# Sinkhorn attention into a gated MLP on one core: all of q turned on TensorE in bf16, eight shared load buffers, a new order of units

## The chip, the core and the metric

The kernel runs on one core of a Trainium2 chip. Five engines work side by side, each on its own queue of instructions: TensorE (PE in the profile, with its weight loads on a row of their own, PEld), VectorE (DVE), ScalarE (ACT), GpSimd (POOL) and SyncE (SP, which here only issues DMAs). The metric is the device time of one execution in microseconds (us); lower is better.

## What is computed

```python
# attention: batch 4, 8 heads, 768 rows, 64 columns; sort_net gives one 8x8 matrix per head
P = sort_net
for _ in range(5):                                   # five Sinkhorn rounds
    P = exp(P - max);  P /= sum over rows;  P /= sum over columns
k_sorted = einsum('bhij,bhjcd->bhicd', P, k_blocks)  # 8 blocks of 96 rows, mixed by P
v_sorted = einsum('bhij,bhjcd->bhicd', P, v_blocks)
attn = softmax(q_blocks @ k_sorted.T / 8)            # inside a block: 96 x 96
x = (attn @ v_sorted) as (4, 768, 512)               # the 8 heads side by side
# gated MLP with a spatial unit
h = relu(x @ w_in)                                   # 512 -> 1024
u, v = h[..., :512], h[..., 512:]
v_n = (v - mean) / sqrt(var + 1e-6)
v_s = einsum('ts,bsd->btd', w_spatial, v_n) + b_spatial
out = (u * v_s) @ w_out                              # float32, (4, 768, 512)
```

## The kernel before

The work of the four batches is cut into small *units*, each a function `u_XX`, and the text table `ORDER` (lines 18 to 51) lists every unit in the order in which its instructions are written. Nothing reorders them afterwards: each engine runs its own instructions in this order, and waits between engines are by semaphore. So a unit's place in `ORDER` settles what stands ahead of it on each of the five queues. A unit such as `SC:2:1:0:1` names, after the operation, the PSUM tile that it writes (there are four, `ps0` to `ps3`, of two banks each), the engine that empties it where there is a choice (A for ACT, D for DVE, P for POOL), the batch and the piece. A unit that writes a PSUM tile waits until the tile's last user has emptied it.

The units, in the order of one batch's data:

- `L` loads from DRAM, issued by POOL, with a cast to bf16: `q`, `k` and `v` of a batch (768 KB in bf16 each; batch 0 in two halves), the two halves of `w_in` (`wv`, `wu`), `w_spatial` (`ws`) and `w_out` (`wo`). Each of `q`, `k` and `v` has two buffers of its own. At most eight of POOL's DMAs are in flight: the ninth waits for the first to land.
- `SK` is one Sinkhorn round (DVE and ACT), `PR`, `P0`, `PC` and `PD` spread the result into the mixing matrices `pd`. `DM` runs matmuls on a tile of zeros ahead of the first data.
- `QT` turns two heads of q (128 x 768) to `qT`: twelve matmuls against the identity into an fp32 PSUM tile, and a copy. This is done for batches 0 and 1. For batches 2 and 3, `QP` first copies q into another order (`qp`, one buffer, on POOL or DVE), and `QX` turns all eight heads with one DMA transpose, issued by SP.
- `KT` mixes and turns k; `VT` and `VB` mix, turn and turn back v of batch 0; for batches 1 to 3, `VM` mixes v into the one tile `vm`, and `VC` has SP copy it by eight DMAs into `vb` (two buffers).
- `SC` computes scores of two heads and four blocks, with the exp on ACT; `AT` multiplies them by `vb`, and DVE normalizes into `x_sb`.
- `XT` (PE, batches 0 and 1) or `XD` (a DMA transpose, batches 2 and 3) turns the attention's output to `xT`.
- `VP` and `UP` are the two halves of `x @ w_in`; `ST`, `LN` and `LA` are the layer norm of v on DVE (with two small operations on ACT); `WT` turns `w_spatial`; `SP` is the spatial product, whose result DVE adds to the bias (`z`); `GT` multiplies by u (POOL or DVE); `OP` is the last product, `OE` empties it and `OS` stores it.
- `CK`, `CF` and `LF` compute and read one flag that says whether the inputs need the general path, a second version of the whole program behind a branch at the end, which is not taken here. `BH` marks the place of a branch hint.

Of the kernel before, what the change touches and what calls it, by code (L numbers as in the profile page):

```python
# [65 lines left out]
def kernel(  # L66
# [12 lines left out]
    nc = tc.nc  # L79
# [19 lines left out]
    ld = ctx.enter_context(tc.tile_pool(name="ld", bufs=2))  # L99
# [54 lines left out]

    def u_L(what, *a):
        if what in ("q", "k", "v"):
            b, lo, hi = (int(x) for x in a)
            src = {"q": q, "k": k, "v": v}[what]  # L160
            if (what, b) not in st:
                st[what, b] = ld.tile([128, H, G * D], BF16, name=f"{what}_in", tag=what)
# [4 lines left out]
        elif what == "wv":  # L167
            nc.gpsimd.dma_start(
                out=w_in_sb[:, :, DH:DFF], in_=moe_w_in.rearrange("(kc p) f -> p kc f", p=128)[:, :, DH:DFF])
        elif what == "wu":  # L170
            nc.gpsimd.dma_start(
                out=w_in_sb[:, :, 0:DH], in_=moe_w_in.rearrange("(kc p) f -> p kc f", p=128)[:, :, 0:DH])
        elif what == "ws":
            nc.gpsimd.dma_start(out=wsp_nat, in_=moe_w_spatial.rearrange("(c p) s -> p c s", p=128))
        elif what == "wo":
            nc.gpsimd.dma_start(out=w_out_sb, in_=moe_w_out.rearrange("(fc p) n -> p fc n", p=128))
# [112 lines left out]
    def natural(eng, dst, t):  # L289
        copy(eng, dst[:, 0:S].rearrange("p (x g) -> p x g", g=G), t[:, 0:S].rearrange("p (g x) -> p x g", g=G))  # L290
# [96 lines left out]
    def s_block(bank, ii, in_runs):  # L387
        if in_runs:
            return bank[:, 0:HW].rearrange("p (g x) -> p g x", g=G)[:, :, ii * TB:(ii + 1) * TB]
        return bank[:, ii * BLK:(ii + 1) * BLK]  # L390

    def u_SC(ps, b, hp, ih):
# [3 lines left out]
        for ii in range(NI):  # L396
            i = ih * NI + ii
            for hh in range(2):
                rows = slice(hh * 64, hh * 64 + 64)
                nc.tensor.matmul(  # L400
                    s_block(t[:, hh], ii, ("qp", b) in st),
                    lhsT=kT[rows, i * BLK:i * BLK + 128], rhs=q_block(b, hp, rows, i),
                    start=True, stop=True,
                )
        e, scores = e_tile(b, hp, ih), t[0:BLK, :, 0:NI * BLK]
        if ("qp", b) in st:
            e = e.rearrange("p h (x g) -> p h x g", g=G)
            scores = scores.rearrange("p h (g x) -> p h x g", g=G)
        nc.scalar.activation(out=e, in_=scores, func=AF.Exp, scale=scale)  # L409
# [307 lines left out]
```

## Time and profile before

| what | value |
|---|---|
| time before, median of 3 runs | 171.51 us (171.31 to 175.47) |
| the profiled execution | 171.02 us, of which the profile's span is 169.2 us |
| PE busy | 147.8 us (87%) |
| DVE, ACT, POOL busy | 118.3, 81.4, 43.9 us |
| loaded from DRAM, stored | 24.78 MB, 6.29 MB |

The span starts with the first instruction and ends with the last; some 1.8 us of the execution lie outside it. "Idle before" in the profile is the time that an engine stood still ahead of an instruction, with what it waited for behind the arrow. PEclk is the clock that TensorE was granted, as a share of full speed. `SPq` or `DVEq` means the engine's queue, not its work. The page of the profile merges matmuls that follow each other: `x12` is twelve of them.

### The profile page before, as it was taken

What the parts mean: (1) busy time and instruction counts of PE and PEld (TensorE: products, weight loads), DVE (VectorE), ACT (ScalarE), POOL (GpSimd) and SP (SyncE); (2) the same over time, 40 slices, a digit from 0 to 9 for tenths busy, and PEclk for the clock granted to TensorE, in tenths of its full rate; (3) what the DMA queues carried; (4) which work ended last, traced back from release to release, by engine and by line L of the source; (5) the groups of instructions that cost most, each with busy time, mean ns of one, the idle gap of its engine ahead of it and who ended that gap; (6) DMA issues with size and microseconds to landing.
All of it is one profiled execution on the core that took longest, in us unless ns stands there. A gap on an engine that the chain in (4) does not pass through costs nothing.

```text
span 169.2 us, 3790 instructions
## 1 busy us (share of the span) xinstructions
PE 147.8 (87%) x1559; PEld 90.8 (54%) x1559; DVE 118.3 (70%) x261; ACT 81.4 (48%) x113; POOL 43.9 (26%) x49
## 2 busy tenths in 40 slices
PE   7828989999799899819689999999999999999840
PEld 5627867765576666413255655555566545555310
DVE  3855699889599936149478697868959689546630
ACT  3227696796776653304737343688650045600120
POOL 7957320000009945318000030000003600006000
PEclk9995699999999999975999999999999999999996
DMA  2999999999996999914999926891309903311063
GB/s 24 173 195 204 208 205 203 207 212 205 248 267 98 120 158 157 113 17 53 188 254 224 204 48 34 242 237 28 124 6 114 318 0 124 124 62 67 4 252 128
DMA packets 33589, 24.74 MB, mean 146 GB/s; under 512 B 13472, under 2 KB 30368, under 8 KB 33568
## 3 DMA queue, kind: packets, MB, share of 16 engines
q0 software_dynamic: 14896, 12.19, 47.5%
q1 hardware_dynamic: 18672, 12.28, 32.9%
q8 instruction: 13, 0.21, 0.5%
q14 instruction: 8, 0.07, 0.1%
HBM read 24.78 MB, written 6.29 MB: 184 GB/s over the span
## 4 chain that ended last, share of the span: by engine, by line
PE 49%; DMA 24%; DVE 10%; ACT 6%; issue 3%; SPq 2%; POOL 2%; DVEq 0%; ACTq 0%; POOLq 0%
PE ps L558 12%; PE ps L584 10%; DMA qT<-qp 10%; PE ps L546 8%; DMA vb<-vm 7%; PE ps L503 7%; DMA v_in<-in_v_dram 6%; PE ps L336 3%; PE ps L448 3%; PE ps L400 3%; DVE v_sb L532 2%; DVE x_sb L456 2%; ACT ex L409 2%; SPq L376 2%; DVE z L564 2%
## 5 line engine op out<-in xcount | busy, mean ns | idle before, releaser
L574 POOL TENSOR_TENSOR gt<-z,u_sb 128x768 bf16<-128x768 f32 x10 | 16.4, 1641 | 76.4 <-DVE rec_all L455 46.4
L558 PE MATMUL ps<-wspT,v_sb 128*128 128x384 bf16 x192 | 33.0, 326 | 0.1
L409 ACT ACTIVATE ex<-ps 96x768 bf16<-96x768 f32 x32 | 24.3, 806 | 9.0 <-PE ps L400 9.0
L558 PEld LDWEIGHTS <-v_sb 128*128 128x128 bf16 x192 | 18.2, 98 | 11.8
L503 PE MATMUL ps<-w_in_sb,xT 128*128 128x512 bf16 x96 | 24.1, 400 | 0.0
L546 PE MATMUL ps<-xT,w_in_sb 128*128 128x384 bf16 x128 | 23.3, 326 | 0.6 <-DVE x_sb L456 0.6
L564 DVE TENSOR_TENSOR z<-ps,b_bc 128x768 f32<-128x768 f32 x16 | 15.3, 955 | 11.9 <-PE ps L558 11.9
L584 PE MATMUL ps<-w_out_sb,gt 128*128 128x512 bf16 x96 | 22.7, 381 | 0.7 <-DVE gt L574 0.7
L456 DVE TENSOR_TENSOR x_sb<-ps,rec_all 96x512 bf16<-96x512 f32 x32 | 22.0, 687 | 1.1
L110 ACT COPY o_sb<-ps 128x1024 f32<-128x1024 f32 (+1 forms) x11 | 9.7, 895 | 21.9 <-PE ps L584 18.2
L116 ACT ACTIVATE v_sb<-ps 128x1024 bf16<-128x1024 f32 x8 | 8.2, 1023 | 23.5 <-PE ps L503 23.5
L520 DVE BATCH_NORM_STATS2 stats<-v_sb 128x6 f32<-128x512 bf16 x24 | 16.2, 674 | 1.0 <-ACT v_sb L116 0.9
L546 PEld LDWEIGHTS <-w_in_sb 128*128 128x128 bf16 x128 | 11.6, 98 | 8.4 <-DVE x_sb L456 1.1
L448 PE MATMUL ps<-vb,ex 96*128 96x65 bf16 x256 | 12.5, 193 | 3.1 <-DMA vb<-vm 3.0
L503 PEld LDWEIGHTS <-xT 128*128 128x128 bf16 x96 | 9.4, 101 | 10.8 <-issue 1.7
L584 PEld LDWEIGHTS <-gt 128*128 128x128 bf16 x96 | 8.9, 98 | 11.3 <-DVE gt L574 1.1
L448 PEld LDWEIGHTS <-ex 96*128 96x128 bf16 x256 | 10.7, 97 | 6.9 <-issue 3.3
L116 ACT ACTIVATE u_sb<-ps 128x768 bf16<-128x768 f32 x13 | 10.5, 811 | 7.3 <-PE ps L546 7.3
L400 PE MATMUL ps<-qT,kt 64*128 64x96 bf16 x256 | 10.1, 215 | 4.6 <-DVE z L564 4.1
L400 PEld LDWEIGHTS <-kt 64*128 64x128 bf16 x256 | 7.0, 100 | 9.8 <-issue 5.2
L110 ACT CAST kt<-ps 128x768 bf16<-128x768 f32 x12 | 9.2, 803 | 5.9 <-PE ps L336 5.9
L314 POOL COPY qp<-q_in 128x768 bf16<-128x768 bf16 x5 | 4.2, 871 | 28.4 <-DMA q_in<-in_q_dram 28.4
(89 smaller groups left out, 181.8 us busy)
## 6 DMA issues: line engine op xcount, KB each, us to landing
out_dram<-o_sb SPq DMA_DIRECT2D x9, 512.0 KB, 3.6
vb<-vm SPq DMA_DIRECT2D x24, 99.0 KB, 5.4
k_in<-in_k_dram POOLq DMA_DIRECT2D x3, 768.0 KB, 18.4
q_in<-in_q_dram POOLq DMA_DIRECT2D x3, 768.0 KB, 20.8
v_in<-in_v_dram POOLq DMA_DIRECT2D x3, 768.0 KB, 16.4
out_dram<-o_sb SPq DMA_DIRECT2D x6, 256.0 KB, 2.5
wsp_nat<-in_moe_w_spatial_dram POOLq DMA_DIRECT2D x1, 1152.0 KB, 26.6
w_in_sb<-in_moe_w_in_dram POOLq DMA_DIRECT2D x2, 512.0 KB, 14.1
```

The lines of the kernel that those rows point to most:

```text
L110: nc.scalar.copy(out=out, in_=in_)
L116: nc.scalar.activation(out=out, in_=in_, func=AF.Relu)
L400: nc.tensor.matmul(s_block(t[:, hh], ii, ("qp", b) in st), lhsT=kT[rows, i * BLK:i * BLK + 128], rhs=q_block(b, hp, rows, i), start=True, ...
L409: nc.scalar.activation(out=e, in_=scores, func=AF.Exp, scale=scale)
L448: nc.tensor.matmul(t[:, hh, ii * VW:ii * VW + D + 1], lhsT=e[:, c:c + 128], rhs=vb[b % 2][:, ih * NI + ii, 2 * hp + hh, 0:D + 1], start=Tr ...
L456: nc.vector.tensor_mul(out=x_sb[:, hp].rearrange("p i (h d) -> p h i d", h=2), in0=tv[:, :, :, 0:D], in1=_raw_ap(rec, 0, [rec.ap[0], [NI, ...
L503: nc.tensor.matmul(t[:, x, :], lhsT=st["xT", b][:, n // 3, kc, (n % 3) * 128:(n % 3 + 1) * 128], rhs=w_in_sb[:, kc, DH:DFF], start=(kc == ...
L546: nc.tensor.matmul(t[:, x, 0:HW], lhsT=w_in_sb[:, kc, mc * 128:(mc + 1) * 128], rhs=st["xT", b][:, ih, kc, :], start=(kc == 0), stop=(kc = ...
L558: nc.tensor.matmul(t[:, x, 0:HW], lhsT=st["v_sb", b, n][:, mc * 128:(mc + 1) * 128], rhs=wspT[:, 3 * x:3 * x + 3, n, :], start=(n == 0), s ...
L564: nc.vector.tensor_add(out=z.rearrange("p (x c) -> p x c", x=2), in0=t[:, :, 0:HW], in1=b_bc.rearrange("p (x c) -> p x c", x=2),)
L574: eng.tensor_mul(out=gt, in0=st["z", b, mc], in1=st["u", b, mc // 2][:, mc % 2])
L584: nc.tensor.matmul(t[:, x, :], lhsT=st["gt", b, mc][:, (n0 + x) * 128:(n0 + x + 1) * 128], rhs=w_out_sb[:, mc, :], start=(mc == 0), stop=( ...
```

## The change

1. **q.** `QP` and `QX` are used no more. All of q is turned on TensorE, with transposes that write bf16 to PSUM: `QT` for two heads (batch 0), and the new `QQ` for four heads at once, whose copy is 128 x 1536 (batches 1 to 3). All of `SC` now reads q in the order that only batches 2 and 3 had.
2. **Load buffers.** The pool `ld` has eight equal buffers, taken in turn by whatever is loaded: q, k and v of all batches, and `w_spatial`, which is loaded in two halves (`wsa`, `wsb`) and has no tile of its own any more. Batch 0's q, k and v are loaded whole.
3. **Copies in two parts.** `KT` may have its copy done half by DVE and half by ACT (`DA`, `AD`).
4. **Order.** `ORDER` is another: among much else v of batch 1 is loaded ahead of k and q, `SC` and `AT` of a batch stand elsewhere, 9 of the 16 `GT` are on DVE (6 before), the warm-up matmuls are 36 of 512 columns (34 of 256 before), and `CK`, `CF` and `LF` stand at the very end. The attention's output of batches 2 and 3 is turned by DMA as before, one `XD` per half.

```diff
-    ld = ctx.enter_context(tc.tile_pool(name="ld", bufs=2))
+    ld = ctx.enter_context(tc.tile_pool(name="ld", bufs=8))
...
-    wsp_nat = const.tile([128, G, S], BF16, name="wsp_nat")
...
+    def ld_tile(name):
+        return ld.tile([128, H, G * D], BF16, name=name, tag="ld")
...
     def natural(eng, dst, t):
-        copy(eng, dst[:, 0:S].rearrange("p (x g) -> p x g", g=G), t[:, 0:S].rearrange("p (g x) -> p x g", g=G))
+        to = dst[:, 0:S].rearrange("p (x g) -> p x g", g=G)
+        of = t[:, 0:S].rearrange("p (g x) -> p x g", g=G)
+        for n, e in enumerate(eng):
+            x = slice(n * 128 // len(eng), (n + 1) * 128 // len(eng))
+            copy(e, to[:, x], of[:, x])
...
+    def q_turned(t, b, hp):
+        for g in range(G):
+            for hh in range(2):
+                nc.tensor.transpose(
+                    t[hh * 64:hh * 64 + 64, g * 128:(g + 1) * 128],
+                    st["q", b][:, 2 * hp + hh, g * D:(g + 1) * D], ident)
+
     def u_QT(ps, eng, b, hp):
+        b, hp = int(b), int(hp)
+        t = ps_tile(ps, BF16)
+        q_turned(t[:, 0], b, hp)
+        copy(eng, q_tile(b)[:, hp * S:(hp + 1) * S], t[:, 0, 0:S])
+
+    def u_QQ(ps, eng, b, hp):
+        b, hp = int(b), int(hp)
+        t = ps_tile(ps, BF16)
+        for x in range(2):
+            q_turned(t[:, x], b, hp + x)
+        copy(eng, q_tile(b)[:, hp * S:(hp + 2) * S].rearrange("p (k c) -> p k c", k=2), t[:, :, 0:S])
...
 ORDER = """
-CO S0 L:q:0:0:4 IV:0 IV:1 ID DM:0:18:256 L:k:0:0:4 SK:0 MA SK:1 MB L:q:0:4:8 IV:2 L:k:0:4:8 DM:1:16:256 SK:2 MC SK:3
+S0 CO SK:0 L:q:0:0:8 L:k:0:0:8 L:v:0:0:8 L:v:1:0:8 BH SK:1 SK:2 L:k:1:0:8 ID IV:2 MC IV:0 DM:1:6:512 L:q:1:0:8 SK:3
...
```

Three places show how this moves instructions.

SP's queue, from the start of the program. `vb<-vm` are the eight DMAs of one `VC`, `qT<-qp` is a `QX`, `xT<-x_sb` an `XD`, `out_dram<-o_sb` an `OS`. Before:

```order
L179 DMA p_all<-in_sort_net_dram 32x64
L376 DMA vb_99<-vm 96x1x528 x8
L185 DMA b_bc<-in_moe_b_spatial_dram 128x768
L321 DMA_TRANSPOSE qT<-qp 128x24x128
L376 DMA vb_98<-vm 96x1x528 x8
L599 DMA out_dram<-o_sb 128x2x512
L466 DMA_TRANSPOSE xT<-x_sb 128x16x96
L321 DMA_TRANSPOSE qT<-qp 128x24x128
```

The same queue after the change:

```order
L182 DMA p_all<-in_sort_net_dram 32x64
L403 DMA vb_98<-vm 96x1x528 x8
L188 DMA b_bc<-in_moe_b_spatial_dram 128x768
L403 DMA vb_97<-vm 96x1x528 x8
L610 DMA out_dram<-o_sb 128x2x512
L486 DMA_TRANSPOSE xT<-x_sb 128x16x96
L610 DMA out_dram<-o_sb 128x2x512
L403 DMA vb_98<-vm 96x1x528 x8
```

Both DMA transposes of q are gone, and nothing stands between the bias and the eight copies of batch 2; the first `XD` now stands ahead of all eight copies of batch 3.

DVE's queue around the spatial product of batch 0 and the mixing of batch 2's v. `qp<-q_in` is a `QP` of batch 3, `z` the emptying of an `SP`, `vm` that of a `VM` of batch 2. Before:

```order
L564 TENSOR_TENSOR z<-ps_1306,b_bc 128x768
L520 BN_STATS stats<-v_sb 128x6
L521 BN_AGGR mv<-stats 128x2
L314 COPY qp<-q_in 128x2x6x64
L564 TENSOR_TENSOR z<-ps_1344,b_bc 128x768
L112 CAST vm<-ps_1365 128x2x6x64
L314 COPY qp<-q_in 128x2x6x64
```

The same place after the change:

```order
L575 TENSOR_TENSOR z<-ps_1222,b_bc 128x768
L109 CAST kt_107<-ps_1249 128x384
L109 CAST kt_108<-ps_1264 128x384
L109 CAST kt_104<-ps_1279 128x384
L109 CAST vm<-ps_1346 128x2x6x64
L575 TENSOR_TENSOR z<-ps_1350,b_bc 128x768
```

The copies into `qp`, which had to wait until the DMA transpose of batch 2 had read the only `qp` buffer, are gone from ahead of `z` and `vm`.

ACT's queue where batch 2's and batch 3's v are mixed, after the change: the first two `vm` rows are the last two of batch 2, and the next two belong to batch 3.

```order
L107 CAST vm<-ps_1369 128x2x6x64
L107 CAST vm<-ps_1384 128x2x6x64
L427 ACTIVATE ex_101<-ps_1403 96x768
L427 ACTIVATE ex_102<-ps_1413 96x768
L113 ACTIVATE v_sb<-ps_1438 128x1024
L427 ACTIVATE ex_103<-ps_1449 96x768
L427 ACTIVATE ex_99<-ps_1459 96x768
L113 ACTIVATE u_sb<-ps_1472 128x2x384
L107 CAST vm<-ps_1500 128x2x6x64
L107 CAST vm<-ps_1504 128x2x6x64
L107 COPY o_sb<-ps_1508 128x1024
```

Before, sixteen other ACT instructions stood between the last `vm` of batch 2 and the first of batch 3 on this queue; now there are six. Since `vm` is one tile, the first `vm` row of batch 3 waits until all eight copies `vb<-vm` of batch 2 have landed.

More of the change, by code (lines that the diff above doesn't have):

```diff
@@ L138 @@
     eps_tile = const.tile([128, 1], FP32, name="eps")
-    warm = const.tile([128, 256], BF16, name="warm")
+    warm = const.tile([128, 512], BF16, name="warm")
     w_in_sb = const.tile([128, KC, DFF], BF16, name="w_in_sb")
-    wsp_nat = const.tile([128, G, S], BF16, name="wsp_nat")
     wspT = const.tile([128, G, G, 128], BF16, name="wspT")
@@ L161, in u_L @@
             if (what, b) not in st:
-                st[what, b] = ld.tile([128, H, G * D], BF16, name=f"{what}_in", tag=what)
+                st[what, b] = ld_tile(f"{what}_in")
             nc.gpsimd.dma_start(
@@ L172, in u_L @@
                 out=w_in_sb[:, :, 0:DH], in_=moe_w_in.rearrange("(kc p) f -> p kc f", p=128)[:, :, 0:DH])
-        elif what == "ws":
-            nc.gpsimd.dma_start(out=wsp_nat, in_=moe_w_spatial.rearrange("(c p) s -> p c s", p=128))
+        elif what in ("wsa", "wsb"):
+            c0 = 0 if what == "wsa" else G // 2
+            st["ws", c0 // (G // 2)] = w = ld_tile("ws_in").rearrange("p h c -> p (h c)")[:, 0:G // 2 * S].rearrange(
+                "p (c s) -> p c s", s=S)
+            nc.gpsimd.dma_start(
+                out=w, in_=moe_w_spatial.rearrange("(c p) s -> p c s", p=128)[:, c0:c0 + G // 2])
         elif what == "wo":
@@ L312, in u_QP @@
         if ("qp", b) not in st:
-            st["qp", b] = att.tile([128, HP, G, 2, D], BF16, name="qp", tag="qp", bufs=1)
+            st["qp", b] = ld_tile("qp").rearrange("p h c -> p (h c)").rearrange(
+                "p (k g h d) -> p k g h d", k=HP, g=G, h=2)
         getattr(nc, {"P": "gpsimd", "D": "vector"}[eng]).tensor_copy(
@@ L400, in u_SC @@
                 nc.tensor.matmul(
-                    s_block(t[:, hh], ii, ("qp", b) in st),
-                    lhsT=kT[rows, i * BLK:i * BLK + 128], rhs=q_block(b, hp, rows, i),
+                    t[:, hh, 0:HW].rearrange("p (g x) -> p g x", g=G)[:, :, ii * TB:(ii + 1) * TB],
+                    lhsT=kT[rows, i * BLK:i * BLK + 128], rhs=q_runs(b, hp, rows, i),
                     start=True, stop=True,
                 )
[L405 to L409, printed above, removed]
+        nc.scalar.activation(
+            out=e_tile(b, hp, ih).rearrange("p h (x g) -> p h x g", g=G),
+            in_=t[0:BLK, :, 0:HW].rearrange("p h (g x) -> p h x g", g=G), func=AF.Exp, scale=scale)
     def u_SM(b, hp, ih):
@@ L483, in u_WT @@
         for n in range(G):
-            nc.tensor.transpose(t[:, n * 128:(n + 1) * 128], wsp_nat[:, int(c), n * 128:(n + 1) * 128], ident)
+            nc.tensor.transpose(t[:, n * 128:(n + 1) * 128], st["ws", int(c) // (G // 2)][:, int(c) % (G // 2), n * 128:(n + 1) * 128], ident)
         copy(eng, wspT[:, int(c)].rearrange("p n t -> p (n t)"), t)
-    def u_WX(lo, hi):
-        lo, hi = int(lo), int(hi)
-        nc.sync.dma_start_transpose(
-            out=wspT[:, lo:hi].rearrange("p c n t -> p (c n) t"),
-            in_=wsp_nat[:, lo:hi].rearrange("p c s -> p (c s)"),
-        )
     def u_VP(ps, eng, b, *tiles):
```

76 lines of the change are left out of this document (34 added, 42 removed).

## The prediction

> **What bounds the kernel now.** First the page's shares and its 40 slices of 4.23 us, then busy time by stages that I cut where PE's work changes pace (columns: us, then busy us of PE, PEld, DVE, ACT, POOL, then PE's granted clock, DMA share, GB/s).
>
> ```profile
> PE 147.8 (87%) x1559; PEld 90.8 (54%) x1559; DVE 118.3 (70%) x261; ACT 81.4 (48%) x113; POOL 43.9 (26%) x49
> ...
> PE   7828989999799899819689999999999999999840
> ```
>
> ```profile
> 15.60:28.40 12.80, 12.11 (x249) 10.46 (x250) 9.96 (x20) 10.03 (x14) 3.82 (x5) 0.84 1.29 205
> 38.90:58.60 19.70, 18.32 (x255) 12.54 (x256) 16.90 (x36) 14.01 (x20) 8.01 (x9) 1.00 1.04 187
> 71.40:85.20 13.80, 7.57 (x56) 3.56 (x56) 8.06 (x14) 4.93 (x6) 4.25 (x4) 0.75 0.63 92
> 85.20:132.85 47.65, 47.45 (x486) 27.77 (x485) 38.25 (x74) 24.07 (x33) 3.92 (x3) 1.00 0.73 140
> 132.85:156.57 23.72, 23.72 (x130) 12.43 (x128) 16.29 (x39) 7.21 (x9) 5.93 (x4) 1.00 0.28 107
> ```
>
> PE is the bound nearly everywhere; slices 3 (before the data are there), 18 and 20 (2, 1 and 6 tenths) are the exceptions. Busy time flatters PE (a matmul's record is longer than its share of the stream), so I price units from the chain of work that ended last, where PE runs without a pause (start us, us, line and matmuls).
>
> ```profile
> 32.10 0.75 PE ps L302 x24
> 33.33 0.89 PE ps L302 x24
> 103.84 0.33 PE ps L363 x2
> 106.12 1.64 PE ps L336 x48
> 109.60 0.45 PE ps L400 x16
> 118.20 0.48 PE ps L448 x16
> 127.16 5.85 PE ps L558 x36
> 133.01 5.18 PE ps L503 x24
> 139.92 2.60 PE ps L546 x16
> 142.52 1.73 PE ps L584 x8
> ```
>
> So `SP` costs 1.95 us, `VP` of two tiles and `OP` 1.73, `UP` 1.30, `KT` 0.41, `VM` 0.33, `SC` 0.23, `AT` 0.24, and turning q 0.38 to 0.45 for two heads. With these prices the units in `ORDER` hold 9.0 us of PE work in the stage of 12.8, 16.9 in that of 19.7, 4.6 in that of 13.8 (four `SC`, one `VP`, one `OP`, one `AT`), 46.6 in that of 47.65 and 23.4 in that of 23.72. PE thus loses 3.8 us at the start, 2.8 around 45 us, **9.2 us between 71.4 and 85.2**, and next to nothing after. The chain of work that ended last says what holds it there (start us, us, what):
>
> ```profile
> 58.07 16.11 DMA qT<-qp
> ...
> 75.56 0.52 PE ps L400 x8
> ...
> 78.36 6.69 DMA vb<-vm
> ...
> 85.41 1.73 PE ps L584 x8
> ```
>
> and from the list of who waited for whom (us in total, times, longest):
>
> ```profile
> DVE qp L314 <- DMA qT<-qp: 5.9, 1, 5.9
> ...
> PE ps L448 <- DMA vb<-vm: 3.0, 4, 1.2
> ```
>
> The DMA transpose of batch 2's q takes 16.11 us. Batch 2's scores wait for it, and so does a `QP` of batch 3, since `qp` has one buffer. That copy stands in DVE's queue ahead of a `z` and of the last `vm`, so DVE stands still 5.9 us, `vm` is late, SP's eight copies start late, and the attention waits for those as well: one cause, two waits in a row.
>
> **The change, part by part.** The sum is made on the profiled execution, 171.0 us (span 169.2), half a microsecond under the median of 171.5.
>
> *The hole, −9.2.* Neither `QP` nor `QX` is left, so all that PE loses between 71.4 and 85.2 has no cause any more. What is late next is `VC` of batch 2, and it has a term below. Bounds: −4.2 (only the stretch from 71.4 to 75.56) and −9.2.
>
> *q on PE, +3.3.* Batches 2 and 3 bring eight more pairs of heads. They lie on the path, since PE has no idle time left around them: 8 x 0.41, bounds 8 x 0.38 = 3.0 and 8 x 0.45 = 3.6. They are transposes with bf16 output, which the kernel has already:
>
> ```profile
> L484 PE MATMUL ps<-ident,wsp_nat 128*128 128x128 bf16 x36 | 2.7, 220 | 0.0
> L112 DVE COPY xT<-ps 128x768 bf16<-128x768 bf16 x5 | 2.7, 548 | 0.1
> L112 DVE CAST qT<-ps 128x768 bf16<-128x768 f32 x2 | 1.9, 952 | 0.2 <-PE ps L302 0.2
> L314 DVE COPY qp<-q_in 128x768 bf16<-128x768 bf16 x3 | 2.2, 728 | 5.9 <-DMA qT<-qp 5.9
> L574 DVE TENSOR_TENSOR gt<-z,u_sb 128x768 bf16<-128x768 f32 x6 | 6.6, 1101 | 0.3
> ```
>
> One record is 220 ns long, but 36 of them keep PE busy for 2.7 us: 75 ns each, with others between them. The Trainium skill (TensorE: Matmul & The Clock Gate, Part 4: PE-mode transpose) says otherwise: such a transpose took some 275 ns in one kernel, and does not count as activity for the clock. By its figure the 192 transposes of q would cost 53 us, an estimate from that page, and the sum would be far above the time of today; the trace disagrees, with 75 ns, and a granted clock of 1.00 in the stage from 38.9 to 58.6 in which all 36 lie.
>
> *DVE, +0.5.* On DVE three `QP` (3 x 0.73) and two fp32 copies of q (2 x 0.95) go. Three `QQ` come (1.1 each, twice the 548; ACT empties the other three), two bf16 copies of batch 0's q (2 x 0.55) and three `GT` from POOL (3 x 1.1): 7.7 more against 4.1 less, so 3.6 us more. It is hidden as long as DVE keeps its lead, and in the dense stage it is busy 38.25 of 47.65 us; spread over the program, 3.6 us leave most of that lead. Where it is used up, DVE empties a PSUM tile late and PE waits for the tile. Bounds 0 and 2, about half of the added work.
>
> *Waits for `vb` of batch 1, −1.2.* Two of the four waits in the row above belong to batch 1 and make part of the 2.8 us lost around 45. Now 8 us of PE work (two `VP` and two of half the size, `UP`, four `SC` and smaller ones) stand between the issue of its `VC` and the first `AT`. Bounds −1.5 and 0.
>
> *`vm` is written again sooner, +1.4.* This is the wait that the change adds.
>
> ```profile
> 76.43 5.69 SPq L376 DMA_DIRECT2D vb<-vm  x8
> DMA to landing us min/median/max: 2.7/5.4/6.7
> L110 ACT CAST vm<-ps 128x768 bf16<-128x768 f32 x8 | 6.3, 801 | 3.0 <-PE ps L363 3.0
> ```
>
> Batch 3's first `vm` copy on ACT waits until batch 2's eight DMAs have landed. Behind it in ACT's queue stand two more `vm`, an `OE` and two `UP`; PE waits for `ps1`, which the second `vm` has to empty before `AT:1:2:3:1`. From the end of the last `VM` of batch 2 it takes 0.3 + 0.8 (copy) + 5.7 (issue) + the landing + 1.6 (two copies) = 8.4 us and the landing; PE has 10.0 us of work for it (two `VP`, `SP`, `OP`, `UP`, four `SC`, two `VM`). So PE loses the landing less 1.6: 1.1 with 2.7, 5.1 with 6.7. I take a landing of 3.0, since no load is queued at that time (k and q of batch 3 are issued after the last `GT` of batch 0, as these DMAs end). Bounds 0 and 5.1.
>
> *Loads and start, 0.* Loads land in the order of issue:
>
> ```profile
> 9.83 0.88 POOL L163 DMA_DIRECT2D q_in<-in_q_dram  x1 [0.55 <-DMA k_in<-in_k_dram]
> 13.92 0.82 POOL L174 DMA_DIRECT2D wsp_nat<-in_moe_w_spatial_dram  x1 [1.13 <-DMA k_in<-in_k_dram]
> 15.60 1.49 PE L336 MATMUL ps<-pd,v_in 128*64 128x128 bf16 x24 [0.67 <-DMA v_in<-in_v_dram]
> 50.57 2.48 POOL L314 COPY qp<-q_in 128x768 bf16<-128x768 bf16 x3 [28.44 <-DMA q_in<-in_q_dram]
> ```
>
> The second and fourth half loads are there at 9.83 and 13.92, the fifth at 15.60: some 2.0 us for 384 KB. Whole tensors then land at about 9.8 (q), 13.8 (k) and 17.6 (v), and v's first half is 2.0 later than now. Against that, KT and three `SC` of batch 0 are done by then, and the warm-up runs on to the first `KT`, where the clock was 0.84. Further on, q of batch 1 is due at 29 and is turned at about 30; q of batch 2 has eight loads' worth in front of it as before (50.57), is due at 48 to 50, and is turned at about 49. Bounds: −2.8 (12.80 less DVE's 9.96, which the stage can't beat) and +2.0.
>
> *End, 0.* The last product, the copies and stores are as many as before.
>
> ```profile
> 156.57:169.20 12.63, 5.51 (x25) 2.26 (x24) 4.01 (x6) 1.66 (x3) 0.00 (x0) 0.89 0.34 128
> 160.78 2.67 DMA out_dram<-o_sb
> 164.04 0.59 ACT o_sb L110
> L609 DVE TENSOR_REDUCE ends<-rec_all 96x1 f32<-96x256 f32 x2 | 0.8, 405 | 0.0
> ```
>
> The last `OE` still waits for a store to free one of two `o_sb` buffers, and that sets the end. `CK` (two reductions of 0.41 and small ones, about 2 us on DVE) now stands after the last `GT`, beside 3 us of `OP`; without that cover it would delay one of six copies. Reading the flag last lies beside the last store's 2.7 us. Bounds −0.5 and +1.
>
> Sum: −9.2 + 3.3 + 0.5 − 1.2 + 1.4 = −5.2, so 171.0 − 5.2 = **165.8 us**.
>
> **Rivals.**
>
> *The new waits cost more.* The eight copies land as slowly as their median or worst (5.4 to 6.7, +2.4 to +3.7 on my 1.4), DVE takes its 2, or batch 1's wait stays: 168 to 171. For it: 5.4 is the median. Against: the loads that made it so are over by then.
>
> *The hole was only half q's.* The `vb` wait at 78.36 has its own landing of 6.69; if it stays, 5.0 of the 9.2 stay (75.56 to 85.2 holds 9.6 us for 4.6 of work): 170.8. For it: it is in the chain by itself. Against: it began late only because DVE stood still until 74.2 (58.07 + 16.11), and the new order leaves 10 us for it.
>
> *The copies land like the q transpose (slower than before).* The place is batch 3's first `vm` on ACT. If the eight DMAs meet k and q of batch 3 and drain like the transpose did beside loads (16.11), PE loses 14.5 there instead of 1.4: 178.9. It decides from a landing of 12 us on, where the time passes 174.9. For it: 16.11 was measured with loads in flight. Against: the same kind of copy, with loads in flight, took 6.69.
>
> *Transposes don't overlap.* At 220 ns each, one after another, the 192 would take 42 us instead of 6.6: 201. The page cited above speaks for it; the 75 ns speak against.
>
> **How the numbers follow.** My forecast (161.5 to 168): 0.62. All small terms at their good end, 160 to 161.5: 0.03. New waits dearer: 0.13. Half a hole: 0.12. Copies that drain slowly: 0.08. Transposes in a row: 0.02. The likeliest gives 165.8. The range, 161 to 171, leaves out the last two, the best case and the worst part of the two ahead of them. A change of 2% (below 168.1, above 174.9) is about what a measurement of this kernel can tell from none: faster 0.66, same 0.24, slower 0.10.
>
> **What would show it.** No slice between 60 and 90 us with PE under 8 tenths, and no DVE wait of microseconds there; `QQ` at 0.8 us of PE each; ACT's `vm` waiting for `vb<-vm` for 1 to 3 us near 73; the last `SP` ending near 151.5 and 12.6 us after it. I am wrong if PE stands still for more than 4 us anywhere after 20 us, if q or k of batch 2 lands after 52, or if DVE's work in the middle holds PSUM tiles back over and over.

## The result and the profile after

The changed kernel takes 164.0 us (median of 4 runs, 163.94 to 164.23) against 171.4 (171.31 to 175.47); the ratio is 0.958 (95% interval 0.956 to 0.959). The prediction was 165.8 with a range of 161 to 171. The profiled execution took 163.99 us, of which 162.2 are the span. Executions of the kernel before spread from 168.4 to 175.5 us over all the measurements here and those of the kernel after from 163.9 to 164.5, so whatever is read against the one profiled execution of before (171.02) carries that spread.

The page's busy shares and two rows of its 40 slices (4.06 us each):

```profile
PE 147.9 (91%) x1646; PEld 89.5 (55%) x1657; DVE 117.7 (73%) x265; ACT 84.3 (52%) x118; POOL 33.7 (21%) x39
...
PE   6988999899999979999999999999999999999700
...
PEclk9999999999999999999999999999999999999995
```

PE's row has no deep hole left: slices 18 and 20, which were 1 and 6, are 9, and the lowest digit between the start and the end is a 7, in slice 15. PE's busy time did not grow with the transposes of q (147.8 before). Its idle time shrank, as stretches of both kernels show: first the one before, then the one after (columns as in the prediction).

```profile
13.41:156.57 143.16, 133.92 (x1449) 82.17 (x1445) 106.04 (x208) 75.36 (x102) 33.97 (x29) 0.95 0.84 149
156.57:169.20 12.63, 5.51 (x25) 2.26 (x24) 4.01 (x6) 1.66 (x3) 0.00 (x0) 0.89 0.34 128
```

```profile
13.17:147.80 134.63, 131.39 (x1544) 82.29 (x1554) 103.89 (x198) 77.64 (x105) 24.98 (x22) 1.00 0.76 142
48.00:60.00 12.00, 11.13 (x210) 8.32 (x207) 8.52 (x18) 7.29 (x11) 3.28 (x2) 1.00 1.29 203
62.00:85.00 23.00, 22.80 (x201) 12.59 (x202) 16.69 (x33) 14.79 (x21) 6.09 (x5) 1.00 0.76 127
147.80:162.20 14.40, 5.27 (x25) 2.22 (x23) 4.39 (x16) 2.73 (x5) 0.00 (x0) 0.86 0.42 150
```

Both long stretches run from the first `KT` to the end of the last `SP` unit. This body is 8.5 us shorter and the time ahead of it 0.24, but the time behind it is 1.8 us longer (14.40 against 12.63), which leaves 7.0 of the span. In the body PE's idle time fell from 9.2 to 3.2 us. Its busy time fell too, from 133.9 to 131.4, although more transposes of q are in it: the mean granted clock there was 0.95 before and is 1.00 now.

### The profile page after: what moved, and what is told of

Same layout as the page of the kernel before. It is cut to its first block, busy times and chain, and to the rows that moved or that the text cites. A ratio compares the mean times of both kernels' runs of the same rounds, so it can differ in the third digit from the quotient of the medians.

```text
span 162.2 us, 3967 instructions
## 1 busy us (share of the span) xinstructions
PE 147.9 (91%) x1646; PEld 89.5 (55%) x1657; DVE 117.7 (73%) x265; ACT 84.3 (52%) x118; POOL 33.7 (21%) x39
## 4 chain that ended last, share of the span: by engine, by line
PE 78%; ACT 7%; DVE 6%; DMA 2%; issue 2%; DVEq 0%; ACTq 0%
PE ps L569 20%; PE ps L557 13%; PE ps L514 13%; PE ps L595 11%; PE ps L468 4%; PE ps L422 4%; PE ps L363 3%; PE ps L390 3%; PE ps L307 3%; ACT ex L427 2%; ACT kt L107 2%; PE ps L498 2%; DMA out_dram<-o_sb 1%; PE ps L504 1%; ACT o_sb L107 1%
## 5 line engine op out<-in xcount | busy, mean ns | idle before, releaser
L585 POOL TENSOR_TENSOR gt<-z,u_sb 128x768 bf16<-128x768 f32 x7 | 11.4, 1640 | 92.7 <-DVE z L575 42.1
L514 PE MATMUL ps<-w_in_sb,xT 128*128 128x512 bf16 x89 | 22.2, 379 | 0.4
L595 PE MATMUL ps<-w_out_sb,gt 128*128 128x512 bf16 x93 | 22.0, 379 | 0.2
L113 ACT ACTIVATE v_sb<-ps 128x1024 bf16<-128x1024 f32 (+1 forms) x8 | 7.4, 920 | 17.6 <-PE ps L514 17.6
L557 PEld LDWEIGHTS <-w_in_sb 128*128 128x128 bf16 x128 | 11.8, 98 | 7.6
L595 PEld LDWEIGHTS <-gt 128*128 128x128 bf16 x96 | 9.2, 98 | 10.2
L107 ACT CAST kt<-ps 128x768 bf16<-128x768 f32 (+1 forms) x14 | 8.7, 641 | 7.9 <-PE ps L363 5.5
L468 PE MATMUL ps<-vb,ex 96*128 96x65 bf16 x256 | 11.9, 193 | 0.1
L219 PE MATMUL ps<-warm 128*128 128x512 bf16 x35 | 9.9, 436 | 1.3 <-DVE warm L192 1.3
L422 PE MATMUL ps<-qT,kt 64*128 64x96 bf16 x256 | 9.5, 204 | 1.6 <-ACT kt L107 1.3
L422 PEld LDWEIGHTS <-kt 64*128 64x128 bf16 x256 | 6.2, 94 | 6.9 <-issue 3.8
```

Of the source, the lines that this page charges most:

```text
L107: nc.scalar.copy(out=out, in_=in_)
L113: nc.scalar.activation(out=out, in_=in_, func=AF.Relu)
L422: nc.tensor.matmul(t[:, hh, 0:HW].rearrange("p (g x) -> p g x", g=G)[:, :, ii * TB:(ii + 1) * TB], lhsT=kT[rows, i * BLK:i * BLK + 128], r ...
L468: nc.tensor.matmul(t[:, hh, ii * VW:ii * VW + D + 1], lhsT=e[:, c:c + 128], rhs=vb[b % 2][:, ih * NI + ii, 2 * hp + hh, 0:D + 1], start=Tr ...
L514: nc.tensor.matmul(t[:, x, :], lhsT=st["xT", b][:, n // 3, kc, (n % 3) * 128:(n % 3 + 1) * 128], rhs=w_in_sb[:, kc, DH:DFF], start=(kc == ...
L557: nc.tensor.matmul(t[:, x, 0:HW], lhsT=w_in_sb[:, kc, mc * 128:(mc + 1) * 128], rhs=st["xT", b][:, ih, kc, :], start=(kc == 0), stop=(kc = ...
```

## The experiments

Eleven of the twelve ran on one chip. There the kernel after took 164.28 us (163.99 to 164.54), and the kernel before had medians of 170.5 to 171.1, with single runs from 168.4 to 173.6. The twelfth (the second below) ran on another, where the kernel before had a median of 173.1 (168.4 to 175.3). Differences of less than 2 us against the kernel before therefore say little. The readings below rest on the traces and, but for that twelfth run, on differences between kernels of one chip.

### The old order: which part of the change closes the hole?

**q on TensorE alone.**

```diff
-XT:3:A:1:1:2 GT:P:0:0 VM:1:A:2:1 SP:0:0:1 QX:2:0:4 VM:2:A:2:2
+XT:3:A:1:1:2 GT:P:0:0 QT:1:D:2:0 QT:2:A:2:3 VM:1:A:2:1 SP:0:0:1 QT:3:D:2:2 QT:1:A:2:1 VM:2:A:2:2
```

(All `QP` and `QX` are out, and batch 3's four `QT` stand near its old `QX`)

> The kernel before, with q of batches 2 and 3 turned by eight QT (fp32 PSUM, two heads each) in place of the copies and of the two DMA transposes; nothing else moves. Theory (the transpose of 16.11 us is the one cause of the hole): -9.2 for the hole, +3.3 for eight QT, and 1 to 2 us that PE still waits for vb of batch 2 because only some 5 to 8 us of PE work stand behind the issue of its copies: 166 to 168 us. Rival (the vb wait has a cause of its own): half of the hole stays, 170 to 172. Rival (only the new order brings the gain): no change, 171.4.

Measured: 174.3 us (172.6 to 175.7), ratio 1.024 (0.982 to 1.067). No gain can be seen, and the theory's 166 to 168 is ruled out. From the list of who waited for whom, the queues of POOL and SP, and the chain:

```profile
PE ps L446 <- DMA vb<-vm: 4.1, 6, 1.4
...
73.48 0.94 POOL L161 DMA_DIRECT2D k_in<-in_k_dram  x1
74.41 0.88 POOL L161 DMA_DIRECT2D v_in<-in_v_dram  x1
...
74.28 5.56 SPq L374 DMA_DIRECT2D vb<-vm  x8
...
76.53 6.58 DMA vb<-vm
```

PE no longer waits for a DMA transpose of q, and it stops all the same: the fourth of the eight copies, issued at 76.5, lands 6.6 us later. Two loads were issued just as the copies began. The copies themselves start only 2.2 us earlier than before (74.28 against 76.43), and ahead of them PE had lost 1.9 us waiting for DVE's copies of `qT` to free PSUM tiles.

**The same, with those two loads earlier.**

```diff
-L:q:3:0:8
+L:q:3:0:8 L:k:3:0:8 L:v:3:0:8
```

(and out of their old places, behind `VP:3:A:1:2:3` and `ST:1:5`)

> The kernel before with q of batches 2 and 3 on TensorE (the run that did not get faster, 174.3 us), now with the loads of k and v of batch 3 issued right behind that of q of batch 3 and not at 73.5 and 74.4, just as batch 2's copies to vb start. Nothing else moves. Theory (in the old order the wait for vb took the place of the wait for q, and it is long because those two loads are in flight: the fourth copy landed 6.6 us after its issue): landings of about 3 us, PE's wait of some 3.5 us at 80 to 83 nearly gone, 3 to 4 us less than that run, 168.5 to 171 us. Rival (the copies start too late anyway): within 1.5 us of that run, 172.5 to 175.

Measured: 168.25 us (167.6 to 169.0); the profiled execution took 168.1, that without this edit 173.9, but on another chip. Three rows of the run with it, and then the `OP` behind batch 2's first attention, in the chain without this edit and in the chain with it:

```profile
PE ps L446 <- DMA vb<-vm: 1.1, 2, 0.6
...
73.78 5.30 SPq L374 DMA_DIRECT2D vb<-vm  x8
...
78.84 0.41 PE L446 MATMUL ps<-vb,ex 96*128 96x65 bf16 x8
...
83.46 2.57 PE ps L582 x8
...
79.25 1.73 PE ps L582 x8
```

The copies start half a microsecond earlier, and PE runs the attention of batch 2 at 78.84 without a wait; what is left of `vb` waits (1.1) lies elsewhere. From the first issue of the copies to the end of that `OP` it took 11.75 us without the edit (74.28 to 86.03) and takes 7.20 with it (73.78 to 80.98). So some 4.5 us lie in this stretch, where the loads were moved; the 5.8 between the two times compares two chips. (The same move on one chip is tried below, with the late `VM`.) Whether this kernel is faster than the one before is not shown either: that one took 168.4 to 175.3 on this chip.

**The transposes kept, DVE freed.**

```diff
-SP:2:0:2 ST:1:0 QP:D:3:3 XT:3:A:1:1:2
+SP:2:0:2 ST:1:0 XT:3:A:1:1:2
...
-OS:0:2 QP:P:3:2
+OS:0:2 QP:D:3:3 QP:D:3:0 QP:D:3:1 QP:P:3:2
```

(`QP:D:3:0` and `QP:D:3:1` are out of their old places too)

> The kernel before, with DVE's three copies into qp for batch 3 moved behind the store of batch 0's first output, so that DVE is not blocked by the transpose of batch 2; the transposes stay. Theory (one cause, two waits in a row: vb is late only because DVE stood still): PE waits from 71.4 to 74.2 for qT and no longer for vb, 6 us less, 165 to 166.5 us. Rival (the vb wait is its own): only the z and vm delay of 1.4 goes, 170 us.

Measured: 167.2 us (166.5 to 168.2), ratio 0.988 (0.967 to 1.009), which by itself does not tell it from the kernel before. The profiled execution took 166.5, 4.6 less than the profiled one of before. In these two traces the same work, from the `VP` ahead of batch 2's scores to the end of the `OP` behind its first attention, takes 17.56 us before (69.58 to 87.14) and 13.58 here (69.14 to 82.72): 4.0 less, between the theory's 6 and the rival's 1.4. What PE waits for is not what the theory said:

```profile
70.97 0.51 PE L398 MATMUL ps<-qT,kt 64*128 64x96 bf16 x16
...
77.78 0.19 PE L446 MATMUL ps<-vb,ex 96*128 96x65 bf16 x1 [2.12 <-DMA vb<-vm]
79.23 0.43 PE L446 MATMUL ps<-vb,ex 96*128 96x65 bf16 x5 [1.26 <-DMA vb<-vm]
...
70.65 5.53 SPq L374 DMA_DIRECT2D vb<-vm  x8
...
72.58 6.61 DMA vb<-vm
```

The scores start at 70.97 and wait for nothing: this time the transpose, issued at 57.64, had landed in 12.2 us. PE waits for `vb`, whose copies land 6.6 us after their issue, beside the loads of k and v of batch 3, issued at 71.39 and 72.32. So the traces show two things that held batch 2's attention back: DVE blocked by the single `qp` buffer, which made the copies start at 76.43 and not at 70.65, and the loads beside them. That q is turned by a DMA need not hold it back, as long as the transpose lands in time. Here it did, by 1.1 us. With the 16.11 us of before it would have landed at 73.75, 2.8 us behind the start of these scores, and no run shows why it took less. So how many microseconds each part is worth stays open.

### The new order: is the DMA transpose bad there too?

```diff
-SC:1:1:0:1 QQ:2:A:2:2 AT:3:1:1:0 AT:0:1:3:1 SP:1:0:3
+SC:1:1:0:1 QP:P:2:2 QP:P:2:3 AT:3:1:1:0 AT:0:1:3:1 SP:1:0:3 QP:D:2:0 QP:D:2:1 QX:2:0:4
```

(`QQ:1:A:2:0` is out too; in the same way for batch 3, with its `QX` ahead of `AT:0:2:2:0`)

> The kernel after, with q of batches 2 and 3 copied (POOL and DVE) and turned by two DMA transposes again, the order otherwise the new one. Theory (the DMA transpose is what costs): PE loses its 2.9 us of transposes and gets a hole of 6 to 10 us back near 59 to 69, 167 to 172 us. Rival (the new order by itself hides the transposes): 161 to 164.

Measured: 177.8 us (176.7 to 178.7), ratio 1.050 (1.031 to 1.070): 13.6 us above the kernel after, and outside what I had written on the high side. Two pieces of its chain and two of PE's instructions:

```profile
55.56 8.68 DMA qT<-qp
...
98.88 4.63 DMA xT<-x_sb
...
64.37 0.50 PE L423 MATMUL ps<-qT,kt 64*128 64x96 bf16 x8 [2.93 <-DMA qT<-qp]
...
103.55 0.61 PE L515 MATMUL ps<-w_in_sb,xT 128*128 128x512 bf16 x1 [4.21 <-DMA xT<-x_sb]
```

Batch 2 pays directly. Batch 3 pays through SP's queue: its `QX` holds SP from 95.16 to 98.78, so that the transpose of the attention's output behind it starts at 98.88 and PE waits 4.2 us for `xT`. The copies into `qp` cost something as well: ahead of batch 2's scores PE waits 1.8 us for an `xT` copy that stands behind two `QP` on DVE, and 1.2 us for a `wspT` copy behind DVE's layer norm, whose last two `LA` take 0.61 us each there and 0.36 in the kernel after. Behind the waits the granted clock was 0.84 (60 to 72) and 0.79 (95 to 106), against 1.00 in the kernel after. The 13.6 us are not broken down further. At these places the copies and transposes have no room, so the new order, as it stands, needs q on TensorE.

### The wait on vm that the change adds

**A yardstick.** 

> The kernel after, unchanged, as the yardstick of this chip for the three that follow: 164 us, and a spread of less than 0.5 us.

Measured: 164.28 us, as told above. In this second execution of the same kernel PE did wait for batch 3's `vm` ahead of batch 2's attention; in the first one it did not:

```profile
75.17 0.40 PE L468 MATMUL ps<-vb,ex 96*128 96x65 bf16 x8 [0.26 <-ACT vm L107]
```

**The last VM of batch 2 one spatial product later.**

```diff
-VM:2:A:2:0 SP:1:0:0
+SP:1:0:0 VM:2:A:2:0
```

> The kernel after, with the last VM of batch 2 moved behind the spatial product that followed it (1.95 us of PE work later), so that all eight copies to vb start some 2 us later; PE's later work keeps its place. Theory (the wait of batch 3's first vm for those copies is hidden with nothing to spare: the second vm copy ended at 74.91 and AT:1:2:3:1 began at 74.97): 1.4 to 2.0 us more than the kernel after. Rival (there is slack, and my term of 1.4 was wrong as a mechanism): within 0.3 us of it.

Measured: 172.56 us (171.9 to 173.2), 8.3 more than the kernel after, and above the kernel before (ratio 1.011, 1.005 to 1.016). Neither theory allowed for that. First the kernel after (SP's copies, POOL's loads, PE's `VM` and ACT's first `vm` of batch 3, PE's attention of batch 2), then the moved one:

```profile
65.61 5.30 SPq L403 DMA_DIRECT2D vb<-vm  x8
...
70.47 0.94 POOL L162 DMA_DIRECT2D k_in<-in_k_dram  x1
71.41 0.88 POOL L162 DMA_DIRECT2D q_in<-in_q_dram  x1
...
72.39 0.81 PE L390 MATMUL ps<-v_in,pd 128*128 128x384 bf16 x4
...
73.41 1.50 ACT L107 CAST vm<-ps 128x768 bf16<-128x768 f32 x2 [1.28 <-PE ps L390]
...
74.97 0.40 PE L468 MATMUL ps<-vb,ex 96*128 96x65 bf16 x8
```

```profile
67.47 5.42 SPq L403 DMA_DIRECT2D vb<-vm  x8
...
70.06 0.94 POOL L162 DMA_DIRECT2D k_in<-in_k_dram  x1
70.99 0.88 POOL L162 DMA_DIRECT2D q_in<-in_q_dram  x1
...
72.19 6.52 DMA vb<-vm
...
78.93 1.50 ACT L107 CAST vm<-ps 128x768 bf16<-128x768 f32 x2 [6.10 <-DMA vb<-vm]
...
80.48 0.60 PE L468 MATMUL ps<-vb,ex 96*128 96x65 bf16 x8 [4.86 <-ACT vm L107]
```

In the kernel after, the copies are issued until 70.91, and the first load starts at 70.47: they just pass each other, and the last copy lands 2.9 us after the start of its issue. With the copies 1.9 us later, the last three of the eight go out behind the first load and land 6.4 to 6.5 us after their issue; ACT stands still for 6.1 us, and PE behind it. The attention starts 5.5 us later (80.48 against 74.97), and the rest is lost behind it. The work from there to the next spatial product takes 10.17 us in the kernel after (first two rows) and 13.10 in the moved one (last two; the last figures but two are the granted clock):

```profile
74.97:79.11 4.14, 4.14 (x45) 2.77 (x45) 3.35 (x8) 2.73 (x4) 0.00 (x0) 1.00 1.25 182
79.11:85.14 6.03, 5.98 (x64) 3.36 (x64) 5.83 (x13) 3.76 (x7) 0.00 (x0) 1.00 0.95 190
```

```profile
80.48:85.36 4.88, 4.88 (x29) 2.75 (x29) 2.24 (x6) 2.48 (x3) 0.00 (x0) 0.50 0.64 164
85.36:93.58 8.22, 8.17 (x81) 4.57 (x80) 7.20 (x16) 3.97 (x7) 0.00 (x0) 0.93 0.00 0
```

Behind the 4.9 us of standing idle, PE is granted half its clock for 4.9 us, where it is the bound: 5.5 us are lost up to the attention and 2.9 behind it.

**The same, with two vm tiles, and the same with the loads out of the way.**

```diff
-    vm = const.tile([128, G, H, VW], BF16, name="vm")
+    vm = [const.tile([128, G, H, VW], BF16, name=f"vm{n}") for n in range(2)]
...
```

(Batch `b` writes and copies `vm[b % 2]`, and to make room `gt` has five buffers, not six, which it shares with `vT`; the late `VM` stays)

> The kernel with the late VM (172.56 us), now with two vm tiles taken in turn by the batches, so that batch 3's first vm has nothing to wait for (vT and gt share five buffers to make room; nothing else moves). Theory (the whole loss of 8.3 us is the write to the one vm tile, behind which ACT's queue and PE stand): back to 164 to 165.5 us. Rival (PE's attention would have waited for the same landing in vb anyway): 169 to 172.

```diff
-L:v:3:0:8
+L:v:3:0:8 L:k:3:0:8 L:q:3:0:8
...
```

(Both loads are out of their old places, there is one `vm` tile, and the late `VM` stays)

> The kernel with the late VM (172.56 us, one vm tile), with the loads of k and q of batch 3 issued right behind that of v of batch 3 (about 36 us) and not at 70, so that none is in flight when the copies to vb drain. Theory (contention: in that kernel the last copies landed 5.8 us after the last issue, at 78.7, because both loads were issued at 70.1 and 71.0): the last copy lands about 3 us after its issue, and PE loses 2 to 3 us against the kernel after, 166 to 167.5. Rival (the copies are slow by themselves): 171 to 173.

Measured: 164.8 us (164.6 to 165.0) with two tiles, ratio 0.971 (0.964 to 0.977); 166.1 (165.8 to 166.6) with early loads, ratio 0.979 (0.971 to 0.986). Both theories hold. PE's `VM` and ACT's first `vm` of batch 3 with two tiles:

```profile
73.16 0.81 PE L390 MATMUL ps<-v_in,pd 128*128 128x384 bf16 x4
...
73.68 1.50 ACT L107 CAST vm<-ps 128x768 bf16<-128x768 f32 x2 [0.79 <-PE ps L390]
```

and, with one tile and early loads, the piece of the chain and the same copy:

```profile
72.49 2.76 DMA vb<-vm
...
75.48 1.50 ACT L107 CAST vm<-ps 128x768 bf16<-128x768 f32 x2 [2.34 <-DMA vb<-vm]
```

With two tiles ACT waits only for PE, and PE's attention is not held by the copies themselves, although the last ones land as late as in the run above: 7.8 of the 8.3 us were the write to the one tile. Without loads in flight the last copy lands in 2.8 us and not in 6.5, and what is left (1.8 us over the kernel after) is the 1.4 to 2.0 of the first theory for the later start alone; the other 6.5 were the loads. The two `VM` rows also show that the landing did hold ACT in the kernel after, though its row names PE: ACT's copy begins 1.02 us behind the start of PE's `VM` there (72.39 to 73.41), and 0.52 with two tiles.

### The start, the end, and PE's last gap

**No warm-up between q and k.**

```diff
-QT:3:A:0:2 DM:2:6:512 PR:3 DM:2:6:512
+QT:3:A:0:2 PR:3
```

> The kernel after, without the twelve warm-up matmuls that stand between the turning of q and the first k of batch 0 (9.9 to 13.2 us); nothing else. Theory (what the change gained at the start is the granted clock: 1.00 from 13.2 to 26.4 against 0.53 from 13.4 to 20.0 before): the clock falls to 0.5 to 0.7 between 13 and 20 us, and the time rises by 1.5 to 2.5 us. Rival (DVE's copies and the loads set that stretch): the clock falls and the time stays within 0.4 us.

Measured: 164.37 us (163.8 to 164.9), against 164.28. The stretch behind the first `KT`, after and without the matmuls:

```profile
13.17:20.00 6.83, 5.88 (x153) 4.86 (x152) 5.33 (x9) 5.57 (x9) 4.07 (x5) 1.00 1.32 204
```

```profile
13.17:20.00 6.83, 6.24 (x129) 4.85 (x126) 5.26 (x9) 5.15 (x8) 4.07 (x5) 0.76 1.32 204
```

The granted clock falls to 0.76, PE's busy time grows by 0.36, and the time moves by 0.1, less than the spread: the rival was right, and the clock of that stretch does not set the time.

**More warm-up in the kernel before.**

```diff
-QT:2:A:0:0 SK:4 QT:3:A:0:2
+QT:2:A:0:0 DM:1:18:256 SK:4 QT:3:A:0:2
```

> The kernel before, with 18 more warm-up matmuls of 256 columns (3.3 us) where PE waits for the second half of q (7.8 to 11.7 us); nothing else. Theory (the granted clock of 0.79 between 13.4 and 28.2 comes from that wait, and costs time because PE is the bound there): clock near 1.00 in that stretch and 1.5 to 2.5 us less, 169 to 170. Rival (DVE and the loads set that stretch): the clock rises and the time stays, 171 to 171.8.

Measured: 171.9 us (171.1 to 173.9), ratio 1.012 (0.991 to 1.033). Inconclusive: the 18 matmuls left PE idle for 3.0 us ahead of q, the clock in the stretch behind stayed low (0.59 from 13.4 to 20.0), and so the case that I wanted to see did not come about.

**The flag read earlier.**

```diff
-LA:3:4 SP:1:3:2
+LA:3:4 CK SP:1:3:2
...
-SP:0:3:1 OP:2:2:4
+SP:0:3:1 CF:2 OP:2:2:4
...
-GT:D:3:0 SP:3:3:3
+GT:D:3:0 LF SP:3:3:3
```

(All three are out of their old places at the end)

> The kernel after, with CK behind the last layer norm, CF behind the third spatial product of batch 3 and LF ahead of the last: as many instructions, earlier. Theory (the end after the last output copy, 6.8 us against 4.6 before, is longer by the reading of the flag): 1 to 2 us less. Rival (the six stores, issued in a row, set the end): within 0.4 us. Rival (the read stops the engines' queues ahead of the last spatial product): 0.5 to 2 us more.

Measured: 164.31 us (164.2 to 164.4), against 164.28. The time is that of the first rival, but the trace shows two effects that cancel:

```profile
145.35 1.89 PE L595 MATMUL ps<-w_out_sb,gt 128*128 128x512 bf16 x7 [1.08 <-DVE ends L635]
```

PE waits 1.08 us for the flag's reduction, which holds a PSUM tile that an `OP` needs, and the last `SP` ends at 149.19 and not at 147.80. The time behind it is 13.41 us and not 14.40. So the earlier flag did shorten the end by 1.0, as the theory had it, and lost 1.4 ahead of it. An order that reads the flag early without that wait was not run.

**A spatial product among the k units.**

```diff
-KT:0:DA:2:0 KT:2:A:2:1 GT:P:0:2 QQ:1:A:2:0 SC:0:2:3:0 VM:3:D:2:3 SP:2:0:1 VM:1:A:2:2
+GT:P:0:2 SP:2:0:1 KT:0:DA:2:0 KT:1:A:2:1 QQ:3:A:2:0 SC:0:2:3:0 VM:1:D:2:3 VM:2:A:2:2
```

> The kernel after, with one spatial product of batch 0 moved between the second and the third k unit of batch 2 (the tiles of the units around it renamed to fit). In the kernel after, PE loses some 1.2 us between 55.9 and 60.0, where four k units come in a row and ACT and DVE empty them later than PE fills them. Theory (that loss is on the path): 0.6 to 1.2 us less than the kernel after, 163.1 to 163.7. Rival (what is gained is lost again at the next wait): within 0.3 us of it.

Measured: 166.2 us (166.0 to 167.6), ratio 0.981 (0.971 to 0.990), 1.9 more than the kernel after. Both were wrong. Two stretches of the moved kernel and one of PE's rows:

```profile
48.00:60.00 12.00, 11.90 (x193) 8.47 (x193) 9.03 (x18) 6.14 (x9) 3.28 (x2) 1.00 1.28 201
60.00:72.00 12.00, 9.78 (x109) 5.50 (x104) 5.53 (x9) 7.97 (x11) 3.86 (x3) 1.00 0.27 45
...
64.15 0.48 PE L390 MATMUL ps<-v_in,pd 128*128 128x384 bf16 x2 [1.23 <-ACT ex L427]
```

The gap between 48 and 60 is closed (11.13 busy becomes 11.90). From 60 to 72 PE now stands idle for 2.2 us (0.1 after): where the spatial product no longer stands among them, the `VM` units wait for ACT's exp and copies to free their PSUM tiles.

## Why the prediction was right, and where it was not

*The hole, −9.2: the size was right, the reason half.* From 62 to 85 PE is busy 22.80 of 23.00 us, and priced by units it loses 0.5 there, so the hole gave some 8.7 to 9.1. But "neither `QP` nor `QX` is left, so all that PE loses has no cause any more" is refuted as a reason: in the old order q on TensorE brought no gain that could be seen (174.3), because the wait for `vb` stayed. The step that failed is "one cause, two waits in a row". It left out the loads of batch 3, which were in flight beside the copies to `vb`: with DVE freed PE still waited 3.4 us for `vb` in that place, and with the two loads earlier it waited there for nothing. In the traces freeing DVE took 4.0 us out of that stretch (with a transpose that landed 3.9 us faster) and moving the loads some 4.5. The new order does both at once: `VC` is issued 11 us earlier than before (65.6 against 76.4), and just ahead of the loads, which my `vm` term had counted on. That this held was close to luck: the first load starts 0.4 us before the last copy is issued. My rival "the hole was only half q's" described the old order better than my forecast did, and its argument (the copies' own landing of 6.69) was the one to follow up.

*q on PE, +3.3: right.* The group of transposes in the kernel after (the price in the prediction was two times twelve fp32 matmuls in 0.75 to 0.89):

```profile
L307 PE MATMUL ps<-ident,q_in 128*64 128x128 bf16 x192 | 7.0, 220 | 1.1 <-DMA q_in<-in_q_dram 0.5 <-DVE kt L109 0.3 <-issue 0.3
```

192 transposes keep PE busy 7.0 us, against 4.1 for the 96 matmuls of before: 2.9 more. That is 36 ns each, with others beside them, and the granted clock is 1.00 up to the last `SP`. The figure of some 275 ns that the Trainium skill gives (TensorE: Matmul & The Clock Gate, Part 4: PE-mode transpose) does not add up one by one here, and there is no sign that transposes let the clock fall. No run here has a stretch of transposes alone.

*DVE, +0.5: too small, and for another reason.* DVE's busy time did not grow by 3.6 us, it fell from 118.3 to 117.7: the layer norm's `LA` alone went from 24 of 500 ns to 24 of 403. PE loses 0.87 us of idle time between 48 and 60, where four `KT` in a row are emptied by DVE and ACT; by unit prices 1.2. The one try to close it cost 1.9.

*Waits for `vb` of batch 1, −1.2: right.* None is recorded, and the stretch that lost 2.8 loses some 2, of which 1.2 is the new loss at the `KT`.

*`vm` written again, +1.4: nothing to 0.3, and the bounds were not the right ones.* I had the chain of steps right (ACT's copies at 73.41, over at 74.91, then the attention at 74.97), but each step was a little long. The landing that I took counts from the start of an issue, and I added it to the end of the last one, so 0.6 stood in the sum twice; the eight issues took 5.3 and not 5.7, the first wait next to nothing and not 0.3, and PE had 10.2 of work and not 10.0. With that the wait is hidden by 0.06 in one execution and costs PE 0.26 in the other, where the last copy landed 0.2 later. The upper end (+5.1) and the turning point of my slower rival (a landing of 12 us) were too mild, though: starting the copies 1.9 us later, with a landing of 6.5, cost 8.3. A later start also meets the loads, and PE pays for standing idle a second time by the clock behind it, which my sum left out. As a mechanism that rival stood on the right place; the change escapes it so narrowly that copies that start 1.9 us later already meet it.

*Loads and start, 0: 1.0 too high, inside its bounds.* The first `KT` comes 0.24 us earlier, and up to the first `VP` PE loses 0.8 less by unit prices.

*End, 0: wrong.* The time behind the last `SP` is 14.40 us against 12.63 before, so my sign (12.6 us behind it) failed, and +1.8 lies outside my bounds of −0.5 and +1. The output copies are over 7.6 us behind the last `SP` (8.1 before); what is longer is the time from the last of them to the end of the span, 6.8 us against 4.6. By the pages the six stores of 256 KB at the end took 3.2 us to land in the median, against 2.5. The place of the flag has a share in it (1.0, in the run above); the rest stays open.

An estimate of the whole, with the prediction's unit prices laid on every matmul of both traces: the units of the body cost 3.3 us more (nearly all of it q), and PE loses 19.2 us there before and 7.4 after. Of the 11.8 that it loses less, 0.8 lie ahead of the first `VP`, 1.0 from there to some 60 us (the `KT` and the waits for `vb` of batch 1 together), 9.1 in the stretch of the hole, and 0.9 behind it, for which my sum had no term. With 0.24 ahead of the body and 1.8 more behind it this gives the −7.0. So the number came out 1.8 us from the measured one with some luck: what I had too high (the `vm` term, the start, the stages behind the hole and small ones) was about 3.6, and the end, which I had too low by 1.8, took half of it back.

One thing stays open. The kernel before with its `QP` moved behind and the loads of k and v of batch 3 moved ahead, its DMA transposes kept, was not run; by what each edit brought, it might come near the kernel after without a new order.

## What to carry to other kernels

Before a wait is put down to its slow transfer, ask what else was in flight during it: the same copies landed in 2.8 us or in 6.5, and what decided was the place of two unrelated loads in another engine's queue. When a cause is taken out of a chain, the next link gets the wait unless it is moved as well, so price the change once in the old order and once in the new. And a wait that is hidden by less than a tenth of a microsecond is a cliff, from which PE falls twice (the wait, and the clock behind it): with a second buffer the same late start cost 0.5 us, with earlier loads 1.8, and without either 8.3. What the two would cost where the copies are in time was not run. Last, an equal time is not yet "no effect": the early flag gained 1.0 us and lost it again.

## What the hardware showed that I had not expected

*A DMA transpose has no fixed duration.* The same kind of `QX`, all eight heads of one batch, took 16.11 us for batch 2 (before), 12.2 (with DVE freed) and 8.68 (in the new order), and for batch 3 6.3, 5.9 and 7.2 in the same kernels. In the first two, a load of 768 KB was issued at the same moment as batch 2's transpose, and it took 15.8 and 11.1 us: the two slowed down together.

*DVE's layer norm slows down beside POOL.* Three `LA` in the kernel before, and POOL's multiplication beside them (its copies into `qp` from 50.57 on are in the prediction); then the same three with q on TensorE, where POOL has nothing to do between 44 and 60:

```profile
51.93 2.37 DVE L532 TENSOR_SCALAR v_sb<-v_sb,mv,rstd 128x512 bf16<-128x512 bf16 x3
...
53.03 1.12 POOL L272 TENSOR_TENSOR pd<-mask,prep_sb 128x512 bf16<-128x512 bf16 x1
```

```profile
51.92 1.05 DVE L530 TENSOR_SCALAR v_sb<-v_sb,mv,rstd 128x512 bf16<-128x512 bf16 x3
```

0.79 us each against 0.35; the run with the `QP` moved, which keeps POOL's copies there, shows 0.79 as well. The Trainium skill (SBUF — State Buffer, Who interferes with whom) says why such a pair may collide: the two engines share a pair of ports, and a copy or a scalar operation of VectorE in its faster modes and an instruction of GpSimd hold it in turn. The traces agree as far as they go; no row shows in which mode the layer norm ran. With `QP` gone, this collision is gone too; how much of the kernel's steadier times is due to that wasn't tried.

*What a wait of PE costs behind it.* After an idle stretch of 4.9 us the granted clock was 0.50 for 4.9 us, which cost 2.9 us where PE is the bound; at the start, 0.76 in place of 1.00 for 6.8 us cost nothing that the times show. The hole of before shows the same: of the 9.2 us that it cost by unit prices, 6.2 were idle time (13.80 less 7.57 busy), and the other 3.0 fall on work at a mean granted clock of 0.75.
